# Making the first batch's MLP input channel-major straight from token mixing, and its token-major sums during the first MLP group

## The chip, the cores and the metric

The kernel runs on one core of one Trainium2 chip. Times are device microseconds of one execution. TensorE is called PE, VectorE DVE, ScalarE ACT, GpSimd POOL, as in the profile. Kernels are compared only within the same rounds.

## The reference, cut to what matters

Eight batches of 576 tokens with 512 channels. Attention (local window and eight global tokens) gives x; a residual MLP block follows:

```
a1  = alpha1 * x + beta1
tok = einsum('ts,bsd->btd', w_tok, a1)      # mixes the 576 tokens
u   = x + lam * tok
a2  = alpha2 * u + beta2
ch  = relu(a2 @ w_ch1) @ w_ch2              # 512 -> 2048 -> 512
out = u + lam * ch                          # lam is of the size 0.01
```

## The kernel before

The kernel starts with a prologue: attention of batch 0, loads, transposes of w_tok, token mixing of batch 0. Then come nine MLP groups of 512 tokens each. The attention and the token mixing of batch g+1 are woven between the matmuls of group g.

The MLP needs its input channel-major (UT, channels on partitions); the residual needs u token-major (XR, tokens on partitions). Batch 0 gets both like this:

```python
def tok_tile(b, i):               # one tile of 128 tokens, all 512 channels
    def f():
        ps = pv_ps()              # one of three PSUM banks
        for s in range(4):
            mm(ps, wtT[:, s, cs], XL[par][:, s, :], s == 0, False)
        mm(ps, ... wtT[:, 4, cs] ..., XL4[par], False, True)
        finish_u((b, i), ps)      # DVE: XR += ps
# for batch 0, finish_u also leaves a tail:
#   4 fp32 transposes of XR (PE), then one DVE product with alpha2 -> UT
# XL = x * (lam * alpha1) in bf16, made by POOL head pair by head pair
...
b0_beta(0)                        # POOL, before the last two heads' XL
run(pv[2], ...)
ld_w2(0); ld_w2(1)                # POOL issues the W2 loads
run(pv[3])                        # last head pair; its XL goes to POOL
psr ...                           # 10 matmuls against ones: beta's sums
psb ...                           # bias1 = w_ch1^T beta2: 64 one-column matmuls
b0_beta(1)
for i, (w, f) in enumerate(token_mix(0)):
    f()
    if i > 0:
        late[i - 1]()             # transposes and UT product of the tile before
late[3]()
# group 0:
parts = [(first_attention(1), 4, 94), (token_mix(1), 106, 119)]
```

`weave` lays a part's pieces between MLP matmul slots, from its first to its second number; a group has 128 slots. A tile's add and its fp32 transposes share the tile's PSUM bank.

The softmax here doesn't subtract the row's maximum and nothing guards it: scores larger than these inputs give would overflow.

## Time and profile before

The median was 406.67 us of 3 runs (405.51 to 407.93). In its profile:

| what | before |
|---|---|
| span of the profiled run | 403.6 us |
| common mark: transpose of the alpha/beta rows (8x8) | 41.28 us |
| first MLP matmul | 54.87 us |
| first matmul of group 1 | 102.50 us |

I measure stretches from the common mark. It is the last PE instruction ahead of everything that the change moves on PE, and between runs it falls at 41.3 to 43.3 us, a spread that I leave out in this way. Much of the spread is there without the edit: in after, e2, e5 and e10 PE is already 0.3 to 0.8 us later than here at about 20 us, ahead of everything that moved, and the three latest marks (e1, e3, e6) belong to profiles whose granted clock, the share of full speed that the profile records for PE, was 0.66 from 30 to 40 us instead of 0.83.

Two lines of the page: busy time of PE (share of the span, instructions), and the chain that ended last, by engine:

```profile
PE 375.4 (93%) x3071; PEld 210.2 (52%) x3071; DVE 230.0 (57%) x621; ACT 167.2 (41%) x318; POOL 210.5 (52%) x282
PE 87%; DVE 6%; POOL 2%; DMA 1%; issue 1%; ACT 1%; SPq 0%; DVEq 0%; POOLq 0%
```

The table of stretches, cut at the mark, at the first MLP matmul and at group 1 (length of the stretch, then busy time of each engine with its instructions):

```profile
41.28:54.87 13.59, 10.65 (x141) 7.17 (x140) 7.85 (x21) 2.23 (x6) 10.06 (x14) 1.00 1.65 144
54.87:102.50 47.63, 45.78 (x421) 26.29 (x422) 35.71 (x103) 19.92 (x39) 30.03 (x38) 1.00 1.21 130
```

PE was busy for 10.65 of the 13.59 us of the prologue's last part. By this count only about 3 us there are idle.

The timeline of PE (start, us, engine, line, operation; in brackets the idle time before it and what ended it):

```profile
42.22 0.19 PE L117 MATMUL bank<-RG,G 128*128 128x65 f16 x1 [0.71 <-DVE RG L322]
...
43.07 1.39 PE L117 MATMUL bank<-wtT,ones 128*128 128x512 bf16 x10
44.30 1.34 PE L117 MATMUL bank<-b2c,W 128*128 128x1 bf16 x48
46.12 0.55 PE L117 MATMUL bank<-b2c,W 128*128 128x1 bf16 x16 [0.48 <-issue]
47.22 2.32 PE L117 MATMUL bank<-XL,wtT 128*128 128x512 bf16 x10 [0.55 <-POOL XL L372]
49.38 0.60 PE L418 MATMUL bank<-ident,XR 128*128 128x128 f32 x4
...
53.43 0.66 PE L418 MATMUL bank<-ident,XR 128*128 128x128 f32 x4 [0.42 <-DVE XR L411]
54.87 1.04 PE L117 MATMUL bank<-UT,W 128*128 128x512 bf16 x4 [0.79 <-DVE UT L420]
...
57.64 0.38 PE L556 MATMUL bank<-identb,OT 128*128 128x128 bf16 x4 [0.41 <-DVE QP L560]
...
59.68 0.24 PE L117 MATMUL bank<-OH,UT 128*128 128x8 bf16 x4 [0.32 <-DVE QP L560]
...
102.50 0.59 PE L117 MATMUL bank<-UT,W 128*128 128x512 bf16 x2 [1.11 <-issue]
```

The five waits after the mark and up to the first MLP matmul add up to 0.71 + 0.48 + 0.55 + 0.42 + 0.79 = 2.95 us. The durations of merged groups overlap; the starts give the pace, for instance 217 ns from one 512-column matmul to the next, while the profile lists 379 ns for one. So a wait costs more than the idle time listed for it. Counted from start to start, less the pace, the five cost 0.78 + 0.62 + 0.68 + 0.58 + 0.95 = 3.6 us.

The chain of waits over the same time (start, us, what) passes through POOL:

```profile
41.24 1.26 POOL XL L717
42.57 1.00 POOL XL L372
...
45.26 0.88 POOL W L631
46.16 1.01 POOL XL L372
47.22 2.32 PE bank L117 x10
```

POOL is the last to release token mixing, but PE has other work until 46.67 us. From 41.24 to 47.2 us the chain lies on POOL almost throughout, where PE lost only 0.55 us to it.

### The profile page before, as it was taken

What the parts mean: (1) busy time and instruction counts of PE and PEld (TensorE: products, weight loads), DVE (VectorE), ACT (ScalarE), POOL (GpSimd) and SP (SyncE); (2) the same over time, 40 slices, a digit from 0 to 9 for tenths busy, and PEclk for the clock granted to TensorE, in tenths of its full rate; (3) what the DMA queues carried; (4) which work ended last, traced back from release to release, by engine and by line L of the source; (5) the groups of instructions that cost most, each with busy time, mean ns of one, the idle gap of its engine ahead of it and who ended that gap; (6) DMA issues with size and microseconds to landing.
All of it is one profiled execution on the core that took longest, in us unless ns stands there. A gap on an engine that the chain in (4) does not pass through costs nothing.

```text
span 403.6 us, 8090 instructions
## 1 busy us (share of the span) xinstructions
PE 375.4 (93%) x3071; PEld 210.2 (52%) x3071; DVE 230.0 (57%) x621; ACT 167.2 (41%) x318; POOL 210.5 (52%) x282
## 2 busy tenths in 40 slices
PE   0657889999899999999999999999999999999996
PEld 0546546654565456545654565456545654444443
DVE  3766496578356845794569457845684465113013
ACT  2544328700772078107720781077207810640720
POOL 9534949445964994488447954884340335100000
PEclk9998999999999999999999999999999999999999
DMA  8999999993997999699959998999322003201002
GB/s 172 248 240 237 113 209 131 137 127 91 143 153 144 126 147 127 128 118 148 133 132 117 141 133 136 112 162 159 101 62 70 2 26 82 62 2 78 27 28 78
DMA packets 161690, 48.25 MB, mean 120 GB/s; under 512 B 147530, under 2 KB 154770, under 8 KB 161652
## 3 DMA queue, kind: packets, MB, share of 16 engines
q0 software_dynamic: 98752, 16.99, 62.2%
q1 hardware_dynamic: 62100, 30.36, 39.1%
q8 instruction: 24, 0.39, 0.4%
q10 hardware_dynamic: 800, 0.39, 0.4%
q14 instruction: 14, 0.11, 0.1%
HBM read 39.28 MB, written 9.44 MB: 121 GB/s over the span
## 4 chain that ended last, share of the span: by engine, by line
PE 87%; DVE 6%; POOL 2%; DMA 1%; issue 1%; ACT 1%; SPq 0%; DVEq 0%; POOLq 0%
PE bank L117 86%; DMA SR<-in_k_dram 1%; DVE QP L560 1%; POOL XL L372 1%; PE bank L556 0%; POOL Ve L199 0%; PE bank L418 0%; DVE PT L306 0%; DVE OT L539 0%; POOL XL L717 0%; DVE PT L525 0%; ACT QP L560 0%; DVE QP L576 0%; DVE Kb L539 0%; ACT E L294 0%
## 5 line engine op out<-in xcount | busy, mean ns | idle before, releaser
L117 PE MATMUL bank<-UT,W 128*128 128x512 bf16 x576 | 159.9, 379 | 1.9 <-issue 1.1
L117 PE MATMUL bank<-W,HT 128*128 128x512 bf16 (+2 forms) x592 | 140.2, 373 | 0.0
L484 ACT ACTIVATE HT<-bank,bias 128x512 bf16<-128x512 f32 x144 | 98.7, 686 | 65.4 <-PE bank L117 64.7
L294 ACT ACTIVATE E<-bank 128x416 f16<-128x416 f32 (+1 forms) x96 | 47.4, 513 | 122.8 <-PE bank L117 121.9
L117 PEld LDWEIGHTS <-HT 128*128 128x128 bf16 x592 | 53.4, 97 | 53.3 <-issue 1.6
L372 POOL TENSOR_TENSOR XL<-XR,LA 128x384 bf16<-128x384 f32 x32 | 32.0, 1001 | 86.8 <-DVE XR L354 55.4
L117 PEld LDWEIGHTS <-W 128*128 128x128 bf16 x640 | 50.3, 98 | 27.8 <-issue 2.1
L499 DVE TENSOR_TENSOR OT<-bank,LAM 128x512 f32<-128x512 f32 (+2 forms) x37 | 24.9, 673 | 54.9 <-PE bank L117 54.6
L426 POOL TENSOR_TENSOR UB<-XR,A 128x512 bf16<-128x512 f32 x28 | 35.8, 1289 | 22.3 <-DVE XR L411 15.4
L117 PE MATMUL bank<-RG,G 128*128 128x65 f16 x320 | 43.7, 194 | 3.9 <-DVE RG L322 3.9
L117 PEld LDWEIGHTS <-PT 128*128 128x128 f16 x576 | 33.3, 99 | 20.4 <-issue 3.9
L117 PE MATMUL bank<-Ve,PT 128*128 128x65 f16 x320 | 43.9, 196 | 0.0
L117 PE MATMUL bank<-XL,wtT 128*128 128x512 bf16 (+1 forms) x180 | 41.2, 380 | 0.5 <-POOL XL L372 0.5
L117 PEld LDWEIGHTS <-G 128*128 128x128 f16 x320 | 31.2, 98 | 15.1 <-DVE G L249 0.2
L117 PE MATMUL bank<-QP,KT 128*128 128x144 bf16 (+1 forms) x288 | 33.7, 231 | 4.3 <-ACT E L294 4.1
L117 PEld LDWEIGHTS <-KT 128*128 128x128 bf16 x288 | 25.0, 102 | 21.3 <-issue 4.7
L117 PE MATMUL bank<-Vo,PT 128*128 128x65 f16 x256 | 35.5, 194 | 0.0
L199 POOL DMA_DIRECT2D Ve<-in_v_dram x40 | 34.1, 871 | 1.3 <-DMA HT<-in_moe_w_tok_dram 0.6
L301 DVE TENSOR_TENSOR PGQ<-E,gqm 128x80 f16<-128x80 f16 x64 | 10.2, 201 | 34.5 <-ACT E L294 32.7
L354 DVE TENSOR_TENSOR XR<-bank,rd 128x384 f32<-128x384 f32 x64 | 27.1, 424 | 2.3
L500 DVE TENSOR_TENSOR XR<-OT,XR 128x512 f32<-128x512 f32 (+2 forms) x33 | 26.8, 813 | 1.6
L192 POOL DMA_DIRECT2D Kb<-in_k_dram x30 | 26.8, 894 | 0.1
(131 smaller groups left out, 394.8 us busy)
## 6 DMA issues: line engine op xcount, KB each, us to landing
out_dram<-XR SPq DMA_DIRECT2D x31, 256.0 KB, 2.2
W<-in_moe_w_ch_dram POOLq DMA_DIRECT2D x4, 1024.0 KB, 16.7
Vo<-Ve SPq DMA_DIRECT2D x14, 260.0 KB, 3.8
Ve<-in_v_dram POOLq DMA_DIRECT2D x24, 128.0 KB, 5.4
Kb<-in_k_dram POOLq DMA_DIRECT2D x24, 128.0 KB, 5.9
Qb<-in_q_dram POOLq DMA_DIRECT2D x24, 128.0 KB, 6.6
Ve<-in_v_dram POOLq DMA_DIRECT2D x16, 96.0 KB, 5.4
XR<-in_k_dram SPq DMA_DIRECT2D x3, 512.0 KB, 15.9
```

What stands on the lines that cost most here:

```text
L117: nc.tensor.matmul(out=o, lhsT=l, rhs=r, start=st, stop=sp, skip_group_check=True)
L192: nc.gpsimd.dma_start(out=dst[0:n, c, :].rearrange("p (h d) -> p h d", d=D), in_=src[b, :, c * P : c * P + n, :].rearrange("h p d -> p h d"))
L199: nc.gpsimd.dma_start(out=Ve[b % 2][r0 : r0 + hi - lo, c, :, 0:D], in_=v[b, :, lo:hi, :].rearrange("h p d -> p h d"))
L294: nc.scalar.activation(out=e[:, UOFF[u] : UOFF[u + 1]], in_=ps[:, 0:off], func=AF.Exp, bias=0.0, scale=0.125)
L301: nc.vector.tensor_tensor(out=pg[:, :, c0 : c0 + 16].rearrange("p c (a g) -> p c a g", a=2), in0=gq_in, in1=gq_m, op=ALU.mult)
L354: nc.vector.tensor_tensor(out=xo, in0=pv[:, :, :, 0:64], in1=rb, op=ALU.mult)
L372: xl_eng(b).tensor_tensor(out=XL[b % 2][:, 0:3, 128 * hp : 128 * hp + 128], in0=xo, in1=bass.AP(l.tensor, l.offset, [l.ap[0], [0, 3], [1, ...
L426: nc.gpsimd.tensor_tensor(out=ub, in0=x, in1=A2, op=ALU.mult)
L484: nc.scalar.activation(out=HT[:, ec, :], in_=st["ps"], func=AF.Relu, bias=bias1[:, ec : ec + 1], scale=1.0)
L499: nc.vector.tensor_tensor(out=ot, in0=ps, in1=LAM[:, lo:hi], op=ALU.mult)
L500: nc.vector.tensor_tensor(out=x, in0=ot, in1=x, op=ALU.add)
L560: eng(out=QP[r, hp, a, 0:8, 0:64].rearrange("p t (u j) -> p t u j", j=4), in_=psq[r, 0:512].rearrange("p (j t u) -> p t u j", j=4, t=8),)
```

## The change

The intent: token mixing of batch 0 with the activations stationary gives u channel-major at once, so that the adds, the 16 transposes and the UT products at the end of the prologue go away, and a 128-channel block can start when its own head pair's XL is there. x is added by fp32 matmuls against the identity. The token-major u is needed only when group 0 stores its output, so it is made during group 0. The bias matmuls move to group 0 as well (in group 0 beta2 is added in the UT eviction), POOL's beta products move to an idle time, the W2 issues move behind the XL products, the last head pair's XL goes to DVE, and nine MLP matmuls (three column blocks, three of four channel blocks) run ahead of the last channel block.

```diff
+    def tok_ut(hp):
+        def f():
+            ps = sc_ps()
+            cs = slice(128 * hp, 128 * hp + 128)
+            for s in range(4):
+                mm(ps, XL[0][:, s, cs], wtT[:, s, 64:576], s == 0, False)
+            for i in range(4):
+                mm(ps[:, 128 * i : 128 * i + 128], XR[:, i, cs], ident, False, False)
+            mm(ps, XL4[0][:, cs], wtT[:, 4, 64:576], False, True)
+            nc.scalar.activation(out=UT[0][:, hp, :], in_=ps, func=AF.Identity, bias=b2f[...], scale=a2c[...])
 ... (cut: b2f, the XL engine of head pair 3, no bias in group 0's Relu)
-    b0_beta(0)
-    ld_w2(0)
-    ld_w2(1)
-    run(pv[3])
     psr, psr2 = ...
+    run(tok_ut(0), pv[3])
 ...
-    psb = mlp_ps()      # the 64 bias matmuls
-    for i, (w, f) in enumerate(token_mix(0)): ...
-    late[3]()
+    run(tok_ut(1), tok_ut(2))
+    mlp0 = mlp(0)
+    for f in mlp0[0:9]:
+        f()
+    run(tok_ut(3))
+    ld_w2(0)
+    ld_w2(1)
 ...
-            parts = [(first_attention(1), 4, 94), (token_mix(1), 106, 119)]
+            parts = [(first_attention(1), 12, 94), (token_mix(0), 28, 60), ([(1.0, bias_mm)], 96, 97), (token_mix(1), 106, 119)]
```

More of the change, by code (lines that the diff above doesn't have):

```diff
@@ L171 @@
     b2c = T("b2c", [P, 4], BF16)
+    b2f = T("b2f", [P, 4], FP32)
     ones = T("ones", [P, P], BF16)
@@ L354, in norm, with xl_eng @@
         nc.vector.tensor_tensor(out=xo, in0=pv[:, :, :, 0:64], in1=rb, op=ALU.mult)
-    def xl_eng(b):
-        return nc.gpsimd
+    def xl_eng(b, hp):
+        return nc.vector if (b, hp) == (0, 3) else nc.gpsimd
     def pv_x(b, hp):
@@ L371, in f @@
                     l = LA1[:, 128 * hp : 128 * hp + 128]
-                    xl_eng(b).tensor_tensor(
+                    xl_eng(b, hp).tensor_tensor(
                         out=XL[b % 2][:, 0:3, 128 * hp : 128 * hp + 128],
@@ L397, in f4 @@
             norm(ps, rt, 0, 1, 0, P, xo.rearrange("p (i a d) -> p i a d", i=1, a=2))
-            xl_eng(b).tensor_tensor(out=XL[par][:, 3, cs], in0=xo, in1=LA1[:, cs], op=ALU.mult)
+            xl_eng(b, hp).tensor_tensor(out=XL[par][:, 3, cs], in0=xo, in1=LA1[:, cs], op=ALU.mult)
             r0 = 64 * par
@@ L401, in f4 @@
             norm(ps, rt, 1, 1, r0, r0 + 64, xo.rearrange("p (i a d) -> p i a d", i=1, a=2))
-            xl_eng(b).tensor_tensor(out=XL4[par][r0 : r0 + 64, cs], in0=xo, in1=LA1[r0 : r0 + 64, cs], op=ALU.mult)
+            xl_eng(b, hp).tensor_tensor(out=XL4[par][r0 : r0 + 64, cs], in0=xo, in1=LA1[r0 : r0 + 64, cs], op=ALU.mult)
         return [(0.75, f3), (0.4, f4)]
     nub = [0]
-    late = []
     def finish_u(t, ps):
@@ L414, in finish_u @@
         if t[0] == 0:
-            def tail():
-                for cc in range(4):
-                    nc.tensor.transpose(out=ps[:, 128 * cc : 128 * cc + 128], in_=x[:, 128 * cc : 128 * cc + 128], identity=ident)
-                ab = bass.AP(a2c.tensor, a2c.offset, [a2c.ap[0], [1, 4], [0, 128]])
-                nc.vector.tensor_tensor(out=UT[g % 2][:, :, js], in0=ps.rearrange("p (c t) -> p c t", c=4), in1=ab, op=ALU.mult)
-            late.append(tail)
             return
@@ L438, in f @@
             finish_u((b, i), ps)
+        return (1.1, f)
+    def tok_ut(hp):
[7 more added lines that the diff above has]
+            mm(ps, XL4[0][:, cs], wtT[:, 4, 64:576], False, True)
+            nc.scalar.activation(out=UT[0][:, hp, :], in_=ps, func=AF.Identity, bias=b2f[:, hp : hp + 1], scale=a2c[:, hp : hp + 1])
         return (1.1, f)
@@ L480, in f @@
                 if cc == 0:
-                    st["ps"] = mlp_ps()
-                mm(st["ps"], W1[:, cc, ec * P : (ec + 1) * P], ut[:, cc, :], cc == 0, cc == 3)
+                    st[ec] = mlp_ps()
+                mm(st[ec], W1[:, cc, ec * P : (ec + 1) * P], ut[:, cc, :], cc == 0, cc == 3)
                 if cc == 3:
-                    nc.scalar.activation(out=HT[:, ec, :], in_=st["ps"], func=AF.Relu, bias=bias1[:, ec : ec + 1], scale=1.0)
+                    b_ = bias1[:, ec : ec + 1] if g else 0.0
+                    nc.scalar.activation(out=HT[:, ec, :], in_=st[ec], func=AF.Relu, bias=b_, scale=1.0)
             return f
@@ L507, in w2 @@
             return f
-        for ec in range(16):
-            for cc in range(4):
-                a.append(w1(ec, cc))
+        o = [(ec, cc) for ec in range(16) for cc in range(4)]
+        if g == 0:
+            o = [(ec, cc) for ec in range(3) for cc in range(3)] + [(ec, 3) for ec in range(3)] + o[12:]
+        for ec, cc in o:
+            a.append(w1(ec, cc))
         for j in range(4):
@@ L755 @@
     run(act(fill_pt, 1), tr[2], gl[2], sc[1][0:2], tr[3], gl[3], sc[1][2])
-    run(gk_all(0, gl0_ps), act(b1_begin), act(vo0))
+    run(gk_all(0, gl0_ps), act(b1_begin), act(vo0), act(b0_beta, 0), act(b0_beta, 1))
     nc.vector.tensor_tensor(out=LA1, in0=LA1, in1=LAM, op=ALU.mult)
@@ L764 @@
     nc.tensor.transpose(out=psb[:, 0:8], in_=abr, identity=ident[0:8, 0:8])
-    nc.vector.tensor_copy(out=b2c, in_=psb[:, 0:4])
+    nc.vector.tensor_copy(out=b2f, in_=psb[:, 0:4])
     nc.vector.tensor_copy(out=a2c, in_=psb[:, 4:8])
-    ld_w2(0)
-    ld_w2(1)
-    run(pv[3])
     psr, psr2 = mlp_ps(), mlp_ps()
@@ L779, with bias_mm @@
     nc.scalar.copy(out=wt4o[0:1, 0:64], in_=psr2[0:1, 0:64])
-    psb = mlp_ps()
-    for ec in range(16):
-        for cc in range(4):
-            mm(psb[:, ec : ec + 1], W1[:, cc, ec * P : (ec + 1) * P], b2c[:, cc : cc + 1], cc == 0, cc == 3)
-    nc.vector.tensor_copy(out=bias1, in_=psb[:, 0:16])
-    b0_beta(1)
+    run(tok_ut(1), tok_ut(2))
[5 more added lines that the diff above has]
+    ld_w2(1)
     for hp in range(HP):
         cast_k(hp, g_.tensor_copy)
-    for i, (w, f) in enumerate(token_mix(0)):
-        f()
-        if i > 0:
-            late[i - 1]()
-    late[3]()
     for hp in range(HP):
         cast_q(1, hp, nc.vector.tensor_copy)
+    nc.vector.tensor_copy(out=b2c, in_=b2f)
+    def bias_mm():
+        ps = pv_ps()
+        for ec in range(16):
+            for cc in range(4):
+                mm(ps[:, ec : ec + 1], W1[:, cc, ec * P : (ec + 1) * P], b2c[:, cc : cc + 1], cc == 0, cc == 3)
+        nc.vector.tensor_copy(out=bias1, in_=ps[:, 0:16])
     nc.vector.tensor_scalar(out=hidx, in0=C32[:, 26:30], scalar1=gval[:, 0:1], scalar2=None, op0=ALU.add)
@@ L837 @@
     for g in range(9):
-        base = mlp(g)
+        base = mlp(g) if g else mlp0
         slots = [[] for _ in range(129)]
@@ L867 @@
         if g == 0:
-            parts = [(first_attention(1), 4, 94), (token_mix(1), 106, 119)]
+            for i in range(9):
+                items[i] = lambda i=i: [s() for s in slots[i]]
+        if g == 0:
+            parts = [(first_attention(1), 12, 94), (token_mix(0), 28, 60), ([(1.0, bias_mm)], 96, 97), (token_mix(1), 106, 119)]
         elif g + 1 < NB:
```

## The prediction

> **What bounds the kernel.** TensorE. The page gives PE 93% busy; the chain that ended last is 87% PE. In the table of stretches PE is busy 10.0 of 10 us from 60 to 100 us and without a gap from 150 to 350 us: there every added matmul is paid in full. The change acts on the prologue, before the first MLP matmul at 54.87 us (timeline). Of the 13.6 us from 41.3 to 54.9 us I count about 10 us of PE work: last PV head 0.85, ones-sums 1.3, bias matmuls 1.6 (64 at 25 ns), 20 token-mixing matmuls 4.3 (217 ns apart), 16 fp32 transposes 1.8 (four in 0.44). Only about 3.6 us is idle. The chain there runs over POOL (XL products, DMA issues, two beta products of 1.25 us, the last head's XL at 46.16 to 47.2), then token mixing, and at the end XR add, transposes, UT product (52.7 to 54.8).
>
> **Removed from the prologue.** On POOL, beta products and W2 issues before the last XL (3 us; moved), and that XL itself (goes to DVE); on PE 16 transposes (1.8 us) and the bias matmuls; eight DVE operations of 0.69 us.
>
> **Added.** (a) 16 true fp32 matmuls, XR stationary against the identity. None of that kind is in this trace. The Trainium skill, "FP8 and Floating Point Precision", "TensorE Precision Notes", says true FP32 takes four passes; no run shows it yet. A 128-column bf16 pass is 56 ns, an fp32 transpose with its own weight load 108 ns; I estimate 0.21 to 0.43 us each, 0.3 in the middle: 4.8 us. (b) Four ACT evictions, about 0.69 us each. (c) The 20 bf16 token-mixing matmuls are done twice: again in MLP group 0, where PE is full: +4.3 us. (d) The bias matmuls in group 0: +1.6 us.
>
> **New timeline (estimate).** Ones-sums start at about 41.4, channel block 0 runs 42.8 to 45.1, PV head 3 to 45.9, blocks 1 and 2 to 50.5, nine MLP matmuls to 52.7, block 3 to 55.0, then 0.7 us of waiting for ACT's last eviction: the tenth MLP matmul at about 55.8. Before, nine would have been done at 54.87 + 1.95 = 56.8. So the prologue gains only about 1 us: the wait for POOL is gone, but fp32 matmuls fill it. Group 0 then pays 5.9 us. The stalls of the second batch's transposes near 57.5 and 59.5 (0.4 and 0.3 us) and the 1.1 us wait before group 1 at 101.4 stay.
>
> **Net** about +4.5 us, about 1% slower. Predicted 411.0 us, range 408.3 to 414.3. Chances: faster by over 2% 0.02, within 2% 0.91, slower by over 2% 0.07.
>
> **What the profile would show.** Right: PE's wait for POOL's XL before token mixing vanishes; fp32 matmuls against XR take 0.2 to 0.43 us each; the token-mixing group has 20 more instances; the tenth MLP matmul begins within 1.5 us of 55.8; from there to group 1 it takes about 6 us more; after that only a shift. Wrong: fp32 matmuls at the transposes' 0.11 us would leave about +1.5 us; an MLP start much before 54 would say that the prologue was bound otherwise.
>
> **What would make it wrong.** The cost of the fp32 matmuls is the largest unknown (3 us). Next, stalls in group 0: its attention gets fewer slots while token mixing shares its three PSUM banks, so PE could wait for DVE. On the other side, earlier casts for the second batch may remove the stalls at 57 to 60 us.

## More of the kernel before

The experiments ran on three chips (chip 4 for e1 to e4, 9 for e5 to e8, 8 for e9 to e11), so compare ratios rather than medians.

## The result, and the profile after

The changed kernel took 411.83 us (median of 4 runs, 411.56 to 412.43); the kernel before beside it 407.3 us (4 runs, 405.51 to 408.17). The ratio is 1.0119, with a 95% interval of 1.008 to 1.0158. A ratio is the mean time of one kernel's runs over that of the other's runs of the same rounds, so it is not quite the ratio of the medians. This is slower by about 1.2%, and the interval excludes equality.

The same two lines of the page:

```profile
PE 381.8 (93%) x3107; PEld 214.4 (52%) x3107; DVE 230.0 (56%) x621; ACT 169.5 (41%) x322; POOL 209.4 (51%) x279
PE 85%; DVE 5%; DMA 5%; ACT 2%; issue 1%; SPq 1%; POOL 0%; DVEq 0%; POOLq 0%
```

PE has 6.4 us more to do; the span grew by 6.0 us. The table of stretches, now from the mark to the tenth MLP matmul, and from there to group 1:

```profile
41.90:55.60 13.70, 12.39 (x101) 8.35 (x102) 5.31 (x20) 5.34 (x10) 10.64 (x16) 1.00 1.59 159
55.60:108.07 52.47, 49.98 (x496) 28.96 (x496) 37.03 (x103) 18.70 (x39) 25.69 (x33) 1.00 1.03 113
```

The first line reaches to the tenth matmul, because nine are already done by then. In the kernel before, nine uninterrupted ones would be done at 54.87 + 9 x 0.217 = 56.82 us, 15.54 us after its mark, and from there 45.68 us remain to group 1. So the change won 15.54 - 13.70 = 1.84 us in the prologue and lost 52.47 - 45.68 = 6.79 us in group 0: 4.95 us net. The rest of the kernel runs 301.5 us after group 1's start, against 301.1 before.

The timeline of PE after the change:

```profile
43.29 1.03 PE L117 MATMUL bank<-wtT,XL 128*128 128x512 bf16 x4
44.15 1.05 PE L117 MATMUL bank<-ident,XR 128*128 128x128 f32 x8
45.04 0.38 PE L117 MATMUL bank<-wtT,XL 128*128 128x512 bf16 x1
...
50.06 0.59 PE L117 MATMUL bank<-UT,W 128*128 128x512 bf16 x2
51.09 1.67 PE L117 MATMUL bank<-UT,W 128*128 128x512 bf16 x7 [0.44 <-ACT UT L443]
...
54.35 0.38 PE L117 MATMUL bank<-wtT,XL 128*128 128x512 bf16 x1
55.60 0.81 PE L117 MATMUL bank<-UT,W 128*128 128x512 bf16 x3 [0.87 <-ACT UT L443]
...
58.11 0.38 PE L564 MATMUL bank<-identb,OT 128*128 128x128 bf16 x4 [0.39 <-DVE QP L568]
...
58.55 0.38 PE L117 MATMUL bank<-UT,W 128*128 128x512 bf16 x1
59.02 0.26 PE L117 MATMUL bank<-OH,UT 128*128 128x8 bf16 x4
...
60.44 0.24 PE L117 MATMUL bank<-OH,UT 128*128 128x8 bf16 x4 [0.56 <-DVE QP L568]
...
64.52 1.24 PE L117 MATMUL bank<-XL,wtT 128*128 128x512 bf16 x5
...
66.96 0.24 PE L117 MATMUL bank<-OH,UT 128*128 128x8 bf16 x4 [0.37 <-DVE QP L568]
...
92.47 1.74 PE L117 MATMUL bank<-b2c,W 128*128 128x1 bf16 x64
...
108.07 0.59 PE L117 MATMUL bank<-UT,W 128*128 128x512 bf16 x2 [1.08 <-issue]
```

What to see:

- Four fp32 matmuls take from 44.15 to 45.04 us, 0.222 us each, and appear as two records each. Sixteen are 3.56 us, where the 16 transposes had been 1.76 us.
- The five old waits are gone. Two new ones of 0.44 and 0.87 us stand for ACT's eviction of a UT block, just when a matmul wants it.
- The bias matmuls take 92.47 to 94.08 us, 1.61 us, of group 0. The token-mixing matmuls (the first tile at 64.52) take 4 x 1.08 us more.
- The waits for the second batch's QP copies grew from 0.41 + 0.32 to 0.39 + 0.56 + 0.37 us.

As a sum with the waits from start to start, the prologue is -3.6 (old waits) + 1.6 (new waits, 0.60 and 1.03) + 1.8 (fp32 matmuls for transposes) - 1.6 (bias) = -1.8 us, and -1.84 was measured. (With the listed idle times, -2.95 and +1.31, the sum would be -1.45 us.) In group 0 the waits grew by 0.9 us from start to start; 0.25 of it is the pause before 59.02 us, which is too short to be listed. With 4.33 + 1.61 us of work this is 6.8 us, and 6.79 was measured.

One caution on absolute times: the profiled run of before is one of its quicker ones (405.53 us). In all rounds its runs spread from 404.94 to 408.55 us, and those with a mean granted clock of 0.996 took at most 406.51 us, while those at 0.987 took 406.85 to 408.34. The ratio of the timed runs (1.0119, or 4.85 us of 407.3) is the better measure; the distance from the common mark to group 1 agrees with it. But the ratio mixes runs of different clock: at a mean clock of 0.996 the changed kernel took 411.56 and 411.93 us, and the kernel before 404.94 to 406.51. So the loss may be nearer to the 6.0 us of the two profiles; the 1.0 us in between lies before the mark (0.6) and after group 1's start (0.4).

### The profile page after: what moved, and what is told of

Same layout as the page of the kernel before. It is cut to its first block, busy times and chain, and to the rows that moved or that the text cites. A ratio compares the mean times of both kernels' runs of the same rounds, so it can differ in the third digit from the quotient of the medians.

```text
span 409.6 us, 8164 instructions
## 1 busy us (share of the span) xinstructions
PE 381.8 (93%) x3107; PEld 214.4 (52%) x3107; DVE 230.0 (56%) x621; ACT 169.5 (41%) x322; POOL 209.4 (51%) x279
## 4 chain that ended last, share of the span: by engine, by line
PE 85%; DVE 5%; DMA 5%; ACT 2%; issue 1%; SPq 1%; POOL 0%; DVEq 0%; POOLq 0%
PE bank L117 84%; DMA XR<-in_q_dram 3%; DMA UT<-UB 1%; DMA out_dram<-XR 1%; DVE QP L568 1%; DVE QP L216 1%; DVE XR L506 1%; DVE OT L505 1%; ACT E L295 0%; ACT UT L443 0%; DVE PT L307 0%; ACT HT L490 0%; SPq L419 0%; DVE PT L533 0%; DVE XR L355 0%
## 5 line engine op out<-in xcount | busy, mean ns | idle before, releaser
L490 ACT ACTIVATE HT<-bank,bias 128x512 bf16<-128x512 f32 x128 | 87.9, 687 | 52.4 <-PE bank L117 51.7
L373 POOL TENSOR_TENSOR XL<-XR,LA 128x384 bf16<-128x384 f32 x31 | 31.1, 1004 | 90.6 <-DVE XR L355 63.9
L193 POOL DMA_DIRECT2D Qb<-in_q_dram x30 | 26.8, 892 | 3.3 <-DMA W<-in_moe_w_ch_dram 3.3
```

The costliest lines, as they stand in the source:

```text
L193: nc.gpsimd.dma_start(out=dst[0:n, c, :].rearrange("p (h d) -> p h d", d=D), in_=src[b, :, c * P : c * P + n, :].rearrange("h p d -> p h d"))
L373: xl_eng(b, hp).tensor_tensor(out=XL[b % 2][:, 0:3, 128 * hp : 128 * hp + 128], in0=xo, in1=bass.AP(l.tensor, l.offset, [l.ap[0], [0, 3], ...
L490: nc.scalar.activation(out=HT[:, ec, :], in_=st[ec], func=AF.Relu, bias=b_, scale=1.0)
```

## The experiments

**Theory.** The loss is PE work: the second token mixing and the bias matmuls lie in a group where PE has no gaps, and in the prologue the fp32 matmuls fill most of what the removed waits set free. **Rival A:** the work in group 0 is mostly hidden, and the loss is waiting, above all the fight of two parts for three PSUM banks. **Rival B:** the prologue is bound by evictions and by the XL products, not by PE. **Rival C:** POOL bound the prologue, and its part alone would have been a large gain.

Eleven kernels ran. "Mark to group 1" is read from each profile and is the cleanest measure of the part that was edited, from one profile each; ratios are to the kernel before of the same rounds.

| kernel | median us | ratio (95%) | mark to group 1, us |
|---|---|---|---|
| before (its profile) | 406.67 | 1 | 61.22 |
| changed | 411.83 | 1.0119 (1.0080 to 1.0158) | 66.17 |
| e1 no second sums | 407.62 | 1.0006 (0.9978 to 1.0034) | 61.46 |
| e2 bf16 identity | 409.61 | 1.0052 (1.0025 to 1.0079) | 63.50 |
| e3 sums later | 412.28 | 1.0117 (1.0089 to 1.0146) | 65.78 |
| e4 bias in gap | 411.22 | 1.0100 (1.0069 to 1.0131) | 65.14 |
| e5 POOL only | 405.38 | 0.9958 (0.9930 to 0.9987) | 59.87 |
| e6 order | 406.19 | 0.9980 (0.9952 to 1.0008) | 59.27 |
| e7 early MLP | 405.89 | 0.9967 (0.9941 to 0.9992) | 63.11 (low clock) |
| e8 transpose back | 414.67 | 1.0183 (1.0157 to 1.0209) | 67.25 |
| e9 transpose back, queue mended | 409.76 | 1.0064 (1.0038 to 1.0089) | 63.28 |
| e10 early MLP, casts on ACT | 404.81 | 0.9949 (0.9923 to 0.9976) | 58.66 |
| e11 and group 1 | 403.56 | 0.9913 (0.9887 to 0.9939) | 57.45 |

### e1: without the second sums

```diff
-parts = [(first_attention(1), 12, 94), (token_mix(0), 28, 60), ([(1.0, bias_mm)], 96, 97), ...]
+parts = [(first_attention(1), 12, 94), ([(1.0, bias_mm)], 96, 97), ...]
```

> The changed kernel without the second, token-major token mixing of batch 0 in MLP group 0 (wrong result on purpose: batch 0 loses its token-mixing term in the residual). Theory (the loss is TensorE work laid into a group that is full): 20 matmuls at 217 ns are 4.3 us, and the one 0.37 us wait that this atom's PSUM bank seems to cause near 66.6 us goes too, so about 4.3 to 5.0 us less than the changed kernel: near 407, level with before; from the tenth MLP matmul to group 1 about 47.5 instead of 52.5 us. Rival (the second sums fit into gaps, and the loss is the prologue or the squeezed attention): less than 2 us.

```profile
56.24 0.59 PE L117 MATMUL bank<-UT,W 128*128 128x512 bf16 x2 [0.87 <-ACT UT L443]
...
104.01 0.59 PE L117 MATMUL bank<-UT,W 128*128 128x512 bf16 x2 [1.08 <-issue]
```

The kernel fell to the level of before (1.0006), 4.71 us less between mark and group 1, all of it between the tenth matmul and group 1 (47.77 us instead of 52.47). The 0.37 us wait went with it. The theory's number holds and rival A falls: 4.33 of these 4.71 us are plain matmul work. (The comparison with the reference still passes, probably since lam is of the size 0.01; it is not the asked function all the same.)

### e2: the identity matmuls in bf16

```diff
-mm(ps[:, 128 * i : 128 * i + 128], XR[:, i, cs], ident, False, False)
+mm(ps[:, 128 * i : 128 * i + 128], XL[0][:, i, cs], identb, False, False)
```

> The changed kernel with the 16 fp32 matmuls that add x replaced by bf16 ones (XL and the bf16 identity in place of XR and the fp32 identity: wrong result on purpose, same shape). Theory (the prologue is bound by TensorE after the change): each goes from 0.222 to about 0.056 us, so 2.7 us less, near 409.2; the two waits for the UT evictions (0.44 and 0.87 us) stay. Rival (the prologue is bound by the evictions and by the last head's XL on VectorE): less than 1 us, and new waits appear.

```profile
44.00 0.39 PE L117 MATMUL bank<-identb,XL 128*128 128x128 bf16 x4
44.23 0.38 PE L117 MATMUL bank<-wtT,XL 128*128 128x512 bf16 x1
...
52.77 0.81 PE L117 MATMUL bank<-UT,W 128*128 128x512 bf16 x3 [0.87 <-ACT UT L443]
```

Four of these matmuls now take 0.23 us, where the fp32 ones took 0.89. Measured 2.67 us less between mark and group 1, ratio 1.0052 against 1.0119. The waits of 0.44 and 0.87 us stayed as they were. Rival B falls: after the change the prologue follows PE's work one to one.

### e3: the second sums away from the transposes

```diff
-(token_mix(0), 28, 60)
+(token_mix(0), 60, 76)
```

> The changed kernel with the second token mixing woven into slots 60 to 76 of group 0 instead of 28 to 60, away from the second batch's transposes. Theory: the work stays, only the wait near 66.6 us goes: 0.3 to 0.9 us less than the changed kernel. Rival (most of the loss in group 0 is the fight for the three PSUM banks): 2 us less or more.

The 0.37 us wait went away and mark to group 1 shrank by 0.39 us. The timing cannot resolve so little (1.0117). So the PSUM banks cost some tenths, not more.

### e4: the bias matmuls in the new wait

```diff
-parts = [..., ([(1.0, bias_mm)], 96, 97), ...]
+bias_mm()          # after tok_ut(3) in the prologue
```

> The changed kernel with the 64 bias matmuls (1.6 us) moved from group 0 into the prologue, after the last channel block, where TensorE waits 0.87 us for ScalarE's eviction. Theory: the wait is filled, 0.8 to 0.9 us less than the changed kernel, near 411. Rival (the bias matmuls cost nothing in group 0): up to 0.8 us more.

```profile
54.44 1.74 PE L117 MATMUL bank<-b2c,W 128*128 128x1 bf16 x64
56.04 0.81 PE L117 MATMUL bank<-UT,W 128*128 128x512 bf16 x2
```

The 0.87 us wait (1.03 from start to start) was filled: the tenth matmul came 0.57 us later, the time from there to group 1 fell by 1.60 us (the whole cost of the 64 bias matmuls), 1.03 us net; the ratio went to 1.0100. The direction and the size fit the theory; the timed difference is within its interval.

### e5: the kernel before, with POOL's order alone

```diff
-run(gk_all(0, gl0_ps), act(b1_begin), act(vo0))
+run(gk_all(0, gl0_ps), act(b1_begin), act(vo0), act(b0_beta, 0), act(b0_beta, 1))
...
-ld_w2(0); ld_w2(1); run(pv[3])
+run(pv[3]); ld_w2(0); ld_w2(1)
```

> The kernel before, with GpSimd's order alone changed: both beta products early, the two W2 issues after the last head's XL. Token mixing stays token-major with transposes. Theory: TensorE was nearly full here, so freeing GpSimd only removes the 0.55 us wait for XL before token mixing (bias matmuls end at 46.7, first token mixing 47.2 us): 0.3 to 0.7 us faster than before. Rival (the chain of waits is right, GpSimd bound the prologue and its 3 us are the prize): 2 to 3 us faster.

This was faster than before by about 0.4% (1.7 us by the ratio), 1.35 us on the mark's measure: more than my 0.3 to 0.7, less than rival C's 2 to 3. The 0.55 us wait for XL vanished as expected. So did the 0.48 us pause in the middle of the bias matmuls, which the profile puts to no engine ("issue"); it was also missing in e6 and e10 and came back as 0.87 us in e7.

```profile
45.27 1.74 PE L117 MATMUL bank<-b2c,W 128*128 128x1 bf16 x64
46.87 2.32 PE L117 MATMUL bank<-XL,wtT 128*128 128x512 bf16 x10
```

The packed traces hold a likely cause, which no run tested. The pause always lies between the 48th and the 49th bias matmul. Shortly before, a packet of 16384 bytes lands on the DMA queue q8, of the kind "instruction". Where PE comes to this place 0.37 us after the landing (e7), 1.06 (before) and 1.36 (e11), it pauses 1.01, 0.62 and 0.25 us from start to start; where it comes 1.39 (e10), 1.70 (e5) and 2.24 us (e6) after it, it does not. So PE may be waiting here for its instructions; e5 came to this place about 1 us later than the kernel before. What stands: of the 1.35 us, the wait for XL is 0.68 us from start to start, the size that I had expected, and the pause 0.62, which is not shown to come from POOL's order. Either way it is far less than the 6 us that the chain laid on POOL, and rival C falls.

### e6: the ones-sums ahead of the last PV head

```diff
 # e6: e5, and
 psr, psr2 = ...            # the ten matmuls against ones
+run(pv[3]); ld_w2(0); ld_w2(1)
-xl_eng(b).tensor_tensor(...)       # the last two XL products of a head pair
+xl_eng(b, hp).tensor_tensor(...)   # on DVE for batch 0, head pair 3
```

> As the run before, and the ones-sums issued ahead of the last head's PV matmuls, and that head's last two XL products on VectorE (the first stays on GpSimd). Theory: TensorE works through its 0.7 us wait for RG, and token mixing starts near 45.7 instead of 47.2 us: about 1.3 to 1.8 us faster than before, ratio 0.996. Rival: no more than the run before.

The mark to group 1 fell to 59.27 us, 1.95 less than before, slightly more than expected. The timed ratio of 0.9980 does not show it and is not distinguishable from e5's. The profiled run reached the mark late (43.30 us), at a granted clock of 0.66 between 30 and 40 us (before: 0.83). The edit need not have caused this: e1 and e3 run the changed kernel's code up to the mark, and they reached it at 42.55 and 43.05 us with 0.66 too, where the changed kernel itself had 0.83 and 41.90 us. So the clock of this stretch varies from run to run of the same code.

### e7: MLP halves during the last tile's tail

```diff
 # e7: e6, and
+def w1h(ec, lo, hi):   # one column block of the MLP for tokens lo:hi
+    for cc in range(4):
+        mm(st[ec][:, lo:hi], W1[:, cc, ec * P : (ec + 1) * P], ut[:, cc, lo:hi], cc == 0, cc == 3)
...
+early[0]()             # w1h(0, 0, 256)
 late[3]()
+early[1](); early[2]()
```

> As the run before, and the first three MLP column blocks computed for the first two token tiles (12 matmuls of 256 columns, 1.3 us) while the last tile's add, transposes and eviction run; their other halves follow. No matmul work is added but 12 short ones. Theory: the waits of 0.42 and 0.79 us before the first MLP matmul are filled too: 2.3 to 3.2 us faster than before, ratio 0.993 to 0.994, beating both kernels. Rival (halves cost as much as they fill, or the eviction still ends last): no gain over the run before.

The expected 0.993 to 0.994 did not come (0.9967). In the profile the waits of 0.42 and 0.79 us were gone, but another stood behind them:

```profile
46.90 3.86 PE L117 MATMUL bank<-XL,wtT 128*128 128x512 bf16 x10
...
58.78 0.38 PE L575 MATMUL bank<-identb,OT 128*128 128x128 bf16 x4 [1.50 <-DVE QP L579]
```

The second line is the second batch's transposes, which wait for DVE's QP copies; DVE was still casting that batch's q (1.42 us) when the copies were due. The first line shows that this run also had a low clock: the ten matmuls came 0.369 us apart on average instead of 0.217, and the granted clock was 0.50 from 46.64 to 50.05 us and again from 60.29 to 63.70. It was this kernel's slowest run (408.54 us; its other six took 405.38 to 405.94), so its waits must not be taken at face value. The Trainium skill, "TensorE: Matmul & The Clock Gate", Part 1, says that the array runs at half clock after an idle window of about 3.4 us; the granted 0.50 agrees with half clock, but PE was busy for 2.55 of the 3.42 us before its first drop (longest pause 0.87 us), and no run here shows what set it off.

### e8 and e9: transposing the sums back instead of a second mixing

```diff
 # e8, in tok_ut: keep the fp32 sums, in the place of x
+nc.vector.tensor_copy(out=XR[:, 0:4, cs], in_=ps.rearrange("p (i t) -> p i t", i=4))
 # e8, group 0: 4 fp32 transposes and one copy for each tile; bias as in e4
-(token_mix(0), 28, 60)
+([u_back(i) for i in range(4)], 28, 60)
 # e9: also b2c cast right after a2c, and batch 1's q casts ahead of tok_ut(3)
```

> The changed kernel with the bias matmuls in the prologue's wait (as e4) and the token-major sums of batch 0 no longer multiplied a second time: VectorE keeps the fp32 channel-major sums in x's place, and 16 fp32 transposes (0.108 us each, 1.7 us) bring them back in group 0 instead of 20 matmuls (4.3 us). Right result. Theory: 2.6 us less than e4 (ratio 1.010), so ratio near 1.0035, still not faster than before: the rest is the 3.6 us of fp32 matmuls. Rival (what costs in group 0 is the waiting, not the work): no less than e4.

This miss taught more than a hit. PE's work fell, and yet the kernel became slower than the changed one (1.0183, by the 2% rule "unclear"). The timeline of PE, and that of DVE, in e8:

```profile
58.13 1.75 PE L117 MATMUL bank<-b2c,W 128*128 128x1 bf16 x64 [3.01 <-DVE b2c L805]
```

```profile
55.96 0.69 DVE L444 COPY XR<-bank 128x512 f32<-128x512 f32 x1 [3.75 <-ACT UT L443]
56.57 1.42 DVE L557 CAST OT<-XR 128x512 bf16<-128x512 f32 x4
57.91 0.16 DVE L805 CAST b2c<-b2f 128x4 bf16<-128x4 f32 x1
```

A cast of four columns that depends on nothing recent stood in DVE's queue behind the copy of the last block's sums, which itself waits for PE and ACT, and behind the second batch's q casts (1.42 us). PE waited 3.0 us for it. This profile also has a granted clock of 0.50 from 59.65 to 63.06 us, so the wait need not be the whole loss. The experiment had not tested its question.

> The run that transposed the sums back was slower, not faster: its TensorE waited 3.0 us for b2c, which VectorE had queued behind the copies of the fp32 sums, and then longer for the second batch's QP copies. Here b2c is made at once and the second batch's q casts stand ahead of the last block's copy. If that queue was the cause: the 3.0 us wait is gone and the kernel comes to 1.003 to 1.006 of before. If transposing back is itself dear: still 1.01 or more.

With the queue mended the 3.0 us wait was gone and the ratio 1.0064, at the edge of what I had expected (1.003 to 1.006). Against e4 the mark to group 1 fell by 1.86 us, not 2.6: the wait for the QP copies near 67 us grew from 0.58 to 1.01 us, which is more than half of the difference. So the idea without the double work, with a right result, is still slower than before by 0.6%: the fp32 matmuls remain.

### e10 and e11: a version that beats both

```diff
 # e10: e7, and
-cast_q(1, hp, nc.vector.tensor_copy)
+cast_q(1, hp, nc.scalar.copy)
-(first_attention(1), 4, 94)
+(first_attention(1), 9, 94)
 # e11: also
-(token_mix(1), 106, 119)
+(token_mix(1), 100, 113)
```

> The run with early MLP halves, with the second batch's q casts moved from VectorE (1.4 us just where its QP copies are due) to the idle ScalarE, and that batch's attention started five slots later. In the run before this, TensorE filled the waits ahead of the MLP but then waited 1.50 and 0.77 us for the QP copies, against 0.41 and 0.32 in the kernel before. If that gave the gain back: both waits under 0.5 us, 2.3 to 3.2 us faster than before, ratio 0.992 to 0.994. If not: 0.996 again.

```profile
56.75 0.38 PE L575 MATMUL bank<-identb,OT 128*128 128x128 bf16 x4 [0.60 <-ACT KT L576]
```

The two waits at these places shrank to 0.60 and 0.33 us, the first not below the expected 0.5; the profile puts it to ACT's copy of KT in this run, and to DVE's QP copy in e11. The mark to group 1 fell to 58.66 us, 2.56 less than before. The ratio of 0.9949 is 2.1 us; the expected 0.992 to 0.994 was slightly too good. Since e7's profile was a slow-clock run and the two intervals overlap, that DVE's casts had given e7's gain back is likely, but not proven.

> As the run above, and token mixing of the second batch six slots earlier (100 to 113 instead of 106 to 119), so that its last transposed tile lands before group 1 asks for it. The 1.1 us wait ahead of group 1, which both kernels have, should vanish: 1.0 us less than the run above. If XL of the last head is not ready by then, the wait only moves.

The 1.1 us wait ahead of group 1, common to both kernels, is gone. The line that in the other kernels ends with a wait:

```profile
99.78 0.59 PE L117 MATMUL bank<-UT,W 128*128 128x512 bf16 x2
```

The mark to group 1 is 1.21 us shorter than e10's. The median is 403.56 us, the ratio 0.9913 (0.9887 to 0.9939): the fastest version, token-major as the kernel before.

## Why the prediction was right

It said 411.0 us (408.3 to 414.3) and a net loss of about 4.5 us; measured were 411.83 us and 4.85 us by the ratio. Point by point:

- **PE bounds, and only some 3.6 us of the prologue were idle.** Right. The listed waits were 2.95 us, 3.6 us from start to start, and e2 showed that after the change the prologue follows PE work one to one.
- **fp32 matmuls at 0.21 to 0.43 us, 0.3 in the middle.** They measured 0.222 us. The estimate rested on the Trainium skill, "FP8 and Floating Point Precision", "TensorE Precision Notes", which gives true FP32 four passes; this trace agrees, since 4 x 0.056 = 0.224 us with 0.056 us for a bf16 pass. The weight load that I had feared did not add to it. This term was mis-sized by 16 x 0.08 = 1.2 us; the waits of the next point took a part of that back, and the prologue won 1.84 us and not 1.
- **0.7 us of waiting for ACT's last eviction.** Too little: 0.87 us there, and 0.44 us more for the third block's eviction, which I had not named. The evictions took 0.78 us, not 0.69. The Trainium skill, "ScalarE: Activation LUTs", "What ACT_TABLE_LOAD costs", says that a per-partition pointer operand adds about 93 ns. That agrees and would have mended my estimate: for 128x512 the profile shows 598 ns without one, 687 ns with a bias, 778 ns with a bias and a scale.
- **Group 0 pays 4.3 + 1.6 us.** Right: e1 returned 4.71 us (with 0.37 of waiting), e4 1.60 us. The stretch grew by 6.79 us, 0.9 more than this sum. These are longer waits for the second batch's QP copies (0.59 us as listed, 0.9 from start to start), the risk named at the end of the prediction; e3 showed that 0.39 us come from the place of the second sums.
- **After group 1 only a shift.** Right within 0.4 us.
- **Earlier casts might remove the stalls at 57 to 60 us.** They did not: the casts were done by 50.3 us, and the waits there were 0.39 and 0.56 us against 0.41 and 0.32.

Two errors (fp32 matmuls too dear, waits in group 0 too small) partly cancelled, so the total is closer than its terms; that part is luck.

## What to carry to other kernels

Before removing a wait, add up the busy time of the bounding engine in that stretch: the gain is at most its idle time there (from start to start), whatever the chain through other engines looks like, and any matmul moved or doubled into a full stretch is paid in full. Changing the order of the same work (e5, e10, e11) beat changing the layout at the price of doubled work. When a small operation moves, look at what stands before it in its engine's queue: PE waited 3 us for a four-column cast behind a late copy in e8.

## What the Trainium skill lacked or had wrong

- "TensorE: Matmul & The Clock Gate", "Back-to-back issue gap", gives about 131 ns for each matmul of a sustained stream of weight load and matmul pairs with 512 columns. Here such pairs run at 217 ns (nine MLP matmuls, each with its own weights), as its formula for the isolated gap has it (512/2.4 + 2.5 = 215.8 ns).
- The same section gives about 81 ns for 128 columns. Here eight bf16 transposes of 128 columns, each with its weights, took 0.45 us: 56 ns each, again what the formula gives.
- "FP8 and Floating Point Precision" states the four passes of true FP32 but no time. Here a 128x128 fp32 matmul with its own weights takes 0.222 us, against 0.108 us for an fp32 transpose of the same shape, and leaves two records in the profile.
- No page gives a time for a pause of PE near the landing of an instruction packet. The pause of 0.48 us ("issue") amid 64 one-column matmuls may be one (0.87 us in e7, none in e5, e6 and e10; see e5); no run here tested it.
